# Joining sums and differences of an inverse transform in one VectorE operation per row

## The chip, the cores and the metric

The kernel runs on one core of a Trainium2 chip. The metric is the device time of one execution in microseconds (us), on that core. The core has five engines that work side by side, each through its own queue of instructions in order, and that wait for each other by semaphores: TensorE (PE in the profile, its weight loads PEld), VectorE (DVE), ScalarE (ACT), GpSimd (POOL) and SyncE (SP, which here only issues loads). [...]

## The reference

The kernel computes a long convolution by a gated unit behind it, for a batch of 4, 12800 positions and 128 channels:

```python
u = x * v
y = irfft(rfft(u, n=2*S) * rfft(h_filt, n=2*S))[:, :S, :]
x = x * y
gate_pre[:, t] = sum(conv_w[k] * xp[:, t + k] for k in range(5))   # xp: x with 4 zeros ahead
out = (sigmoid(gate_pre) * (x @ w_val)) @ w_out
```

`h_filt` is a filter that a small network makes from `pos_emb`, times a falling exponential. All values are 32-bit floats.

## The kernel before

The 12800 positions are laid out as J = 2 halves of N1 = 100 by N2 = 64. A position is `n1 * 64 + n2`, and a **row** is one `n2` of one half: 4 batches times 100 positions `n1` (400 elements) for each of the 128 channels. The work has three phases. The first transforms the input along `n1`, the second transforms along `n2`, multiplies with the filter's spectrum and transforms back along `n2` (its results go to the DRAM tensors `c_y` and `c_z`), and the third, which is what the change touches, transforms back along `n1` and does the gated unit. It starts some 680 us into the execution.

In the third phase the 128 rows are worked on in 32 groups of R = 4. The rows pass through these steps, each a small function:

- `y_sum` (L671): two matmuls with the table `inv` give 64 **sums** (S) and 64 **differences** (D) in one PSUM tile `sd`, for two rows at a time.
- `y_copy` (L676): ScalarE copies `sd` to SBUF, `sd_sb`.
- `y_trans` (L683, L685): TensorE transposes it in four pieces (one for each batch) into the PSUM tile `tp`, so that channels lie on the partitions; columns 0 to 63 of a piece are sums, 64 to 127 differences. ScalarE copies the differences, 51 columns of each piece, to `dif` in SBUF.
- `y_join` (L693, L694, L696): VectorE adds, S[i] + D[i] for i = 0 to 50, and subtracts, S[i] - D[i] for i = 1 to 49: a row of 100 values, `yr`. GpSimd multiplies it by the input `xr` and puts it into the tile `ext`.
- `tap` (L710, L713): the convolution over five rows. The first tap is made by ScalarE for a whole group, the four others by VectorE, one for each row of the group, on 1600 elements.
- `sigmoid` (L718), `value` (L725, TensorE, `v_ps`), `gated` (L730, VectorE, `gd`), `project` (L735, TensorE, `o_ps`) and `finish` (L743, ScalarE, `o_sb`, with one store a group).
- `fill_halo` (L651 to L658): ScalarE copies the four rows ahead of a block of four groups into `ext`. For the first block of a half they come from the other end of the signal, moved by one position, so that copy is in pieces.

The order is written out by hand in one loop, one turn for each row. A turn `r` of a group issues: the transposes and the copy of differences of a row that was summed two turns earlier, `value`, the `finish` and `project` of earlier turns, the sums of two rows (every second turn), a tap, a gate, the join, and the copy of a sum; then the halo (r = 1), the next group's first tap (r = 2) or the sigmoid (r = 3). Joins run 8 rows ahead of the taps. The PSUM tiles `tp`, `sd`, `v_ps` and `o_ps` have two buffers each, `dif` and `sd_sb` three, `yr` two.

The positions of a row are not in natural order: `_ORDER` on the host puts 0 to 50 first and then 99 down to 51, as the sums and differences give them, and the host undoes it behind the run.

Of the kernel before, what the change touches and what calls it, by code (L numbers as in the profile page):

```python
# [9 lines left out]
F32 = mybir.dt.float32  # L10
F32R = mybir.dt.float32r
I32 = mybir.dt.int32
AF = mybir.ActivationFunctionType
ALU = mybir.AluOpType
# [9 lines left out]
B, S, D, FO, KC = 4, 12800, 128, 64, 5  # L24
J, N1, N2 = 2, 100, 64
M = N1 * N2
KG = 8
NH = N1 // 2
P0 = 64 - NH
R = 4  # L30
NC1 = N1 // 2 + 1
# [5 lines left out]
def _tables():  # L37
    n1, n2 = np.arange(N1), np.arange(N2)
    k1, k2 = np.arange(N1), np.arange(N2)
    th = 2 * np.pi * (np.outer(n1, 4 * k1 + 1) % (4 * N1)) / (4 * N1)  # L40
    fwd = np.stack([np.cos(th), np.sin(th), -np.cos(th)], 1)

    inv = np.zeros((N1, 3, N2))
    inv[:, 0, :NC1] = (np.cos(th.T) + np.sin(th.T))[:, :NC1] / (2 * M)
    inv[:, 1, :NC1] = (np.cos(th.T) - np.sin(th.T))[:, :NC1] / (2 * M)
    inv[:, 2] = -inv[:, 1]
    flat, inv = inv, np.zeros((128, 3, N2))
    inv[SPREAD] = flat
    ph = (np.outer(4 * k1 + 1, 2 * n2 + 1 - N2)[:, :, None] + 4 * N1 * np.outer(2 * n2 + 1 - N2, k2)[None]) % (8 * M)
    ph = 2 * np.pi * ph / (8 * M)  # L50
    turn = 2 * np.pi * ((N1 - 1) * (4 * k1 + 1) % (8 * N1)) / (8 * N1)

    cos, sin = np.cos(ph[:, :N2 // 2]), np.sin(ph[:, :N2 // 2])
    f = np.stack([np.stack([cos, -sin], 2), np.stack([sin, cos], 2)], 1).reshape(N1, 2 * N2, N2)

    wr, wi = np.cos(ph), np.sin(ph)
    g = np.stack([np.stack([-wi, wr], 1), np.stack([wr, wi], 1)], 2)
    g = g.reshape(N1, 2, 2, 2, N2 // 2, N2).transpose(0, 1, 5, 3, 2, 4).reshape(N1, 2 * N2, 2 * N2)

    ce = 2 * np.pi * ((2 * np.arange(NH)[:, None] + 1 - N1) * (4 * k1 + 1)[None] % (8 * N1)) / (8 * N1)  # L60
    sd = np.zeros((128, 2, 128))
    sd[SPREAD[:, None], :, SPREAD[None]] = np.stack([np.cos(ce), np.sin(ce)], 2)[ROWS[:, 1]]


    f = f.reshape(N1 // 2, 2, 2 * N2, N2).transpose(2, 0, 1, 3).reshape(2 * N2, N1 // 2, 1, 2 * N2)
    g = g.reshape(N1 // 2, 2, 2, N2, 2 * N2).transpose(1, 3, 0, 2, 4).reshape(2 * N2, N1 // 2, 2, 2 * N2)
    w = np.concatenate([f, g], 2)
    be = 2 * np.pi * (np.outer(n2, k2) % N2) / N2
    cb, sb = np.cos(be), np.sin(be)
    dft = np.stack([np.block([[cb, sb], [-sb, cb]]), np.block([[-sb, cb], [-cb, -sb]])], 1)  # L70
    al = 2 * np.pi * np.outer(n2, 4 * k1 + 1) / (4 * M) + turn + np.pi / 4
    tw = np.sqrt(2) * np.tile(np.stack([np.cos(al), np.sin(al)], 1), (2, 1, 1))
    win = np.exp(-0.01 * np.arange(S, dtype=np.float32)).reshape(J, N1, N2)
    win = np.transpose(win, (1, 0, 2))
    tabs = {"fwd": fwd, "sd": sd, "inv": inv, "w": w, "dft": dft, "tw": tw, "win": win, "ident": np.eye(128)}
    return {k: np.ascontiguousarray(a, dtype=np.float32) for k, a in tabs.items()}
# [41 lines left out]
def tile_longconv_gate(  # L118
# [20 lines left out]
    nc = tc.nc  # L139
# [13 lines left out]
    inv = const.tile([128, 3, N2], F32, name="inv")  # L153
# [308 lines left out]
    with tc.tile_pool(name="p2", bufs=1, reuse_waits="tile") as p2, \  # L462
# [89 lines left out]
        with tc.manual_schedule():  # L552
            for p in range(-1, NP + 2):
                now, nxt, old = 0 <= p < NP, p + 1 < NP, 0 <= p - 1 < NP
                if p < 0:
# [6 lines left out]
                    for _ in range(10):  # L562
                        w_ps = ps2.tile([128, 2, BD], F32, name="c_ps", bufs=2)
                        nc.tensor.matmul(
                            out=w_ps[:, 0, 0:2 * D], lhsT=ident, rhs=dft.rearrange("p a k -> p (a k)"), start=True, stop=True)
# [5 lines left out]
                if now:  # L571
                    h = filt_p.pop(p)
# [40 lines left out]
    with tc.tile_pool(name="p3", bufs=1, reuse_waits="tile") as p3, \  # L613
            tc.tile_pool(name="ps3", bufs=1, space=PSUM, reuse_waits="tile") as ps3:
        HALO = KC - 1
# [5 lines left out]
        tails, exts, loads3, sds, tps, gate_sg, gate_gt, outs3 = {}, {}, {}, {}, {}, {}, {}, {}  # L621
# [14 lines left out]
        def place(j, g):  # L636

            if g == NG - 1 and (j, g // EG) not in exts:
                return tails[j], 0
            return exts[j, g // EG], HALO + g % EG * R  # L640
# [5 lines left out]
        def fill_halo(j, q):  # L646
            e = exts[j, q]
            if q == 0:
                t, m = tails[j], N1 // 2
                if j == 0:  # L650
                    nc.vector.memset(e[:, 0:HALO, :, 0:1], 0.0)  # L651
                else:
                    nc.scalar.copy(out=e[:, 0:HALO, :, 0:1], in_=tails[j - 1][:, :, :, m + 1:m + 2])
                nc.scalar.copy(out=e[:, 0:HALO, :, 1:m + 1], in_=t[:, :, :, 0:m])
                nc.scalar.copy(out=e[:, 0:HALO, :, m + 1:N1 - 1], in_=t[:, :, :, m + 2:N1])
                nc.scalar.copy(out=e[:, 0:HALO, :, N1 - 1:N1], in_=t[:, :, :, m:m + 1])
            else:
                nc.scalar.copy(out=e[:, 0:HALO], in_=exts[j, q - 1][:, EG * R:])  # L658

# [19 lines left out]
        def y_trans(s, r):  # L679
            t = sds.pop((s, r))  # L680
            tp = ps3.tile([D, B, 128], F32, name="tp3", bufs=2)
            for b in range(B):
                nc.tensor.transpose(out=tp[:, b], in_=t[:, b], identity=ident)  # L683
            dif = p3.tile([D, B, NC1], F32, name="dif", bufs=3)
            nc.scalar.copy(out=dif, in_=tp[:, :, N2:N2 + NC1])  # L685
            tps[s, r] = tp, dif

        def y_join(s, r):
            tp, dif = tps.pop((s, r))
            j, g = y_order[s]  # L690
            xr = loads3[s].rearrange("d (n b a) -> d n b a", n=R, b=B)[:, r]
            yr = p3.tile([D, B, N1], F32, name="yr", bufs=2)
            nc.vector.tensor_tensor(yr[:, :, 0:NC1], tp[:, :, 0:NC1], dif, op=ALU.add)  # L693
            nc.vector.tensor_tensor(yr[:, :, NC1:N1], tp[:, :, 1:NC1 - 1], dif[:, :, 1:NC1 - 1], op=ALU.subtract)  # L694
            e, r0 = place(j, g)
            nc.gpsimd.tensor_tensor(e[:, r0 + r], yr, xr, op=ALU.mult)  # L696

# [68 lines left out]
        with tc.manual_schedule():  # L766
# [10 lines left out]
            for i in range(-LEAD, (NT - 1) * R):  # L777
                t, r = divmod(i, R)
                s, q = divmod(i + LEAD, R)
                if q == 0 and s < NT:  # L780
                    if 3 <= s + 1 < NT:
                        load_rows(s + 1, (0, 1, 2))
                    j, g = y_order[s]
# [5 lines left out]
                if done:  # L789
                    y_trans(*done)  # L790
# [10 lines left out]
                if done:  # L801
                    y_join(*done)
# [3 lines left out]
                if t + 1 >= 0:  # L806
                    j, g = groups[t + 1]
                    if r == 0 and g == NG - 1:
                        nc.scalar.copy(out=exts[j, g // EG][:, EG * R:], in_=tails[j])
                    if r == 1 and g % EG == 0:  # L810
                        fill_halo(j, g // EG)
                    if r == 2:
                        tap(t + 1, 0)
# [3 lines left out]
            t = NT - 1  # L817
# [24 lines left out]
_INS = ["pos_emb", "w1", "w2", "moe_w_val", "moe_conv_w", "moe_w_out"]  # L842

_OUTS = [((J, D, N2, B, N1), "float32")]
_ORDER = np.concatenate([np.arange(NC1), np.arange(N1 - 1, NC1 - 1, -1)])

# [32 lines left out]
```

## Time and profile before

| | us |
|---|---|
| median of 3 runs | 1068.43 (1066.77 to 1068.98) |
| the profiled execution, by its own time | 1070.6 |
| its span in the trace | 1068.8 |

| engine | busy us | share of the span |
|---|---|---|
| TensorE | 980.4 | 92% |
| VectorE | 972.3 | 91% |
| GpSimd | 747.6 | 70% |
| ScalarE | 624.9 | 58% |

The profile is of one execution. A row of a timeline has the start in us from the start of the span, the length in us, the engine, the line, the operation, what it writes and reads, the size and the count, and in brackets how long the engine sat idle before and what released it. A row of a group has the line, the engine, the operation, the count, then the busy time in us, the mean length in ns, and the idle time before. A row of stretches has, for each engine, its busy us and its instructions, then TensorE's granted clock, the share of the DMA engines and GB/s. An instruction's length includes its way through the engine, so that records of two that follow each other overlap; what a queue can do is read from start to start.

### The profile page before, as it was taken

To read this page: it belongs to the slowest core of one execution; us is meant where nothing else is said; L and a number is where in the kernel's file an instruction comes from. 1 tells how busy PE (TensorE), PEld (TensorE's weight loads), DVE (VectorE), ACT (ScalarE), POOL (GpSimd) and SP (SyncE) were. 2 spreads that over 40 slices of the span, in tenths; PEclk is the share of its full clock that TensorE was granted. 3 is DMA by queue.
4 is the path that set the end of the run, shared out by engine and by line. 5 is a ranking of instruction groups with operands and counts; after the bars stand their busy time and mean duration, and the time that the engine had idled before them with its cause. 6 is when DMAs were issued, how large, how long until landed. Compare 5 with 4: busy or idle time off the path is not lost. (4 is left out here: it accounts for less than half of the span.)

```text
span 1068.8 us, 21559 instructions
## 1 busy us (share of the span) xinstructions
PE 980.4 (92%) x8100; PEld 510.5 (48%) x8100; DVE 972.3 (91%) x1061; ACT 624.9 (58%) x1017; POOL 747.6 (70%) x465
## 2 busy tenths in 40 slices
PE   2768799989998999999999999679999999999996
PEld 0344466656644555455445545334444444444442
DVE  8868999599948999999989999279999999999997
ACT  1545477788862444444434444267677777777774
POOL 2223222222225999999999999689999999999990
PEclk9889899999998999999999999899999999999999
DMA  8999899998989899989989988977788888888813
GB/s 276 372 347 378 329 370 374 384 344 326 388 279 309 317 330 332 334 313 337 344 309 331 345 319 272 342 293 264 273 293 312 270 296 300 278 300 285 298 70 123
DMA packets 97151, 330.16 MB, mean 309 GB/s; under 512 B 12690, under 2 KB 37882, under 8 KB 81050
## 3 DMA queue, kind: packets, MB, share of 16 engines
q1 hardware_dynamic: 41864, 196.96, 54.4%
q10 hardware_dynamic: 49506, 111.30, 26.8%
q0 software_dynamic: 5680, 20.53, 5.0%
q8 instruction: 66, 1.08, 0.4%
q14 instruction: 35, 0.29, 0.1%
HBM read 197.67 MB, written 131.07 MB: 308 GB/s over the span
## 5 line engine op out<-in xcount | busy, mean ns | idle before, releaser
L696 POOL TENSOR_TENSOR ext<-yr,xr 128x400 f32<-128x400 f32 x120 | 308.3, 2570 | 27.3 <-DVE yr L694 24.0
L713 DVE SCALAR_TENSOR_TENSOR gt<-ext,cw,gt 128x1600 f32<-128x1600 f32 (+1 forms) x132 | 240.8, 1824 | 0.1
L400 POOL DMA_DIRECT2D a_u<-st x62 | 33.2, 536 | 225.8 <-ACT st L392 222.0
L392 ACT COPY st<-fp 128x1024 f32<-128x1024 f32 x124 | 125.9, 1030 | 85.4 <-PE fp L391 46.4
L542 POOL TENSOR_TENSOR c_both<-c_raw 128x512 f32<-128x512 f32 x100 | 126.5, 1295 | 9.2 <-DMA c_z<-c_both 6.2
L671 PE MATMUL sd<-ld,inv 128*64 128x512 f32 x512 | 126.4, 612 | 7.2 <-DMA ld<-c_y 6.9
L497 DVE TENSOR_TENSOR va<-z_ps,h_sb 128x2048 f32<-128x2048 f32 x50 | 114.0, 2280 | 18.3 <-PE z_ps L491 18.2
L578 POOL TENSOR_TENSOR va<-va,vb 128x1024 f32<-128x1024 f32 x49 | 117.1, 2390 | 19.0 <-DVE vb L497 18.9
L535 ACT COPY c_raw<-c_ps 128x1024 f32<-128x1024 f32 x50 | 50.8, 1015 | 134.5 <-PE c_ps L530 118.1
L497 DVE TENSOR_TENSOR vb<-z_ps,h_sb 128x2048 f32<-128x2048 f32 x50 | 114.2, 2283 | 11.6 <-POOL va L581 11.6
L676 ACT COPY sd_sb<-sd 128x512 f32<-128x512 f32 x128 | 75.9, 593 | 74.0 <-PE sd L671 62.1
L491 PE MATMUL z_ps<-ld,ld 64*64 64x512 f32 x800 | 111.1, 612 | 8.7 <-DVE vb L497 4.9
L735 PE MATMUL o_ps<-gd,wout 128*128 128x400 f32 x256 | 111.4, 517 | 8.3 <-DVE gd L730 6.8
L391 PE MATMUL fp<-ld,fsd 64*128 64x512 f32 x320 | 90.4, 670 | 28.5 <-DVE ld L342 14.8
L725 PE MATMUL v_ps<-ext,wval 128*128 128x400 f32 x252 | 105.3, 500 | 0.0
L581 POOL TENSOR_TENSOR va<-va,vb 128x1024 f32<-128x1024 f32 x42 | 101.2, 2409 | 0.0
L507 PE MATMUL c_ps<-va,ld 64*64 64x512 f32 x800 | 97.7, 601 | 3.3 <-DVE va L578 1.4
L683 PEld LDWEIGHTS tp<-ident,sd_sb 128*128 128x128 f32 x512 | 58.6, 141 | 77.0 <-PE sd L671 49.6
L513 ACT COPY c_sb<-c_ps 128x1024 f32<-128x1024 f32 x49 | 49.7, 1013 | 58.5 <-PE c_ps L507 58.5
L683 PE MATMUL tp<-ident,sd_sb 128*128 128x128 f32 x512 | 80.3, 280 | 3.8 <-DVE yr L694 2.7
L735 PEld LDWEIGHTS o_ps<-gd,wout 128*128 128x128 f32 x256 | 42.7, 189 | 58.5 <-ACT sd_sb L676 15.4
L730 DVE TENSOR_TENSOR gd<-v_ps,sg 128x400 f32<-128x400 f32 x126 | 70.1, 556 | 0.2 <-ACT sg L718 0.2
(116 smaller groups left out, 1808.8 us busy)
## 6 DMA issues: line engine op xcount, KB each, us to landing
ld<-a_u SPq DMA_DIRECT2D x48, 1024.0 KB
a_u<-st ACTq DMA_DIRECT2D x61, 512.0 KB
xr<-in_xt_dram SPq DMA_DIRECT2D x32, 800.0 KB
c_y<-c_sb ACTq DMA_DIRECT2D x49, 512.0 KB
out_dram<-o_sb ACTq DMA_DIRECT2D x31, 800.0 KB
c_z<-c_both ACTq DMA_DIRECT2D x48, 512.0 KB
ld<-in_xv_dram SPq DMA_DIRECT2D x40, 512.0 KB
ld<-c_y SPq DMA_DIRECT2D x32, 512.0 KB
```

What stands on the lines that cost most here:

```text
L392: nc.scalar.copy(out=st[:, c], in_=fp.rearrange("k j e -> k (j e)"))
L491: nc.tensor.matmul(out=z[half[h], c], lhsT=wk[half[c], 0, half[h]], rhs=a2[half[c], h, j], start=True, stop=True)
L497: nc.vector.tensor_tensor(out, z.rearrange("p (b d) -> p b d", d=D).unsqueeze(1).to_broadcast([128, n, B, D]), h_sb.unsqueeze(2).to_broadc ...
L542: nc.gpsimd.tensor_tensor(both[:, :, m], raw[:, :, 1], raw[:, :, 0], op=op)
L578: (nc.gpsimd if nxt else nc.vector).tensor_tensor(va[:, 0:2], va[:, 0:2], vb[:, 0:2], op=ALU.add)
L581: nc.gpsimd.tensor_tensor(va[:, 2:4], va[:, 2:4], vb[:, 2:4], op=ALU.add)
L671: nc.tensor.matmul(out=to, lhsT=inv[:, 2 if j * m * c else c], rhs=t, start=True, stop=True)
L683: nc.tensor.transpose(out=tp[:, b], in_=t[:, b], identity=ident)
L696: nc.gpsimd.tensor_tensor(e[:, r0 + r], yr, xr, op=ALU.mult)
L713: nc.vector.scalar_tensor_tensor(gt, rows(t, k)[:, cols], cw[:, k:k + 1], gt, op0=ALU.mult, op1=ALU.add)
L725: nc.tensor.matmul(out=v_ps, lhsT=wval, rhs=rows(t)[:, r * ROW:(r + 1) * ROW], start=True, stop=True)
L735: nc.tensor.matmul(out=o_ps, lhsT=wout, rhs=gd, start=True, stop=True)
```

## The change

The differences are copied twice by ScalarE: columns 0 to 49 as they are, and columns 1 to 50 with the sign changed. VectorE then makes the row of 100 in one addition. It reads 50 sums twice over, the second time one column further on, by an access pattern with a step of one column between the two halves, and adds the two halves of `dif`. A row now holds S[i] + D[i] for i = 0 to 49 and S[i] - D[i] for i = 1 to 50. Position 50 therefore comes from a difference instead of a sum, so the table `inv` has the sign of its difference turned, its place in a row is the last (`_ORDER`), and the pieces of the halo's copies are cut one column earlier.

```diff
     inv[:, 1, :NC1] = (np.cos(th.T) - np.sin(th.T))[:, :NC1] / (2 * M)
+    inv[:, 1, NH] *= -1
     inv[:, 2] = -inv[:, 1]
...
-                    nc.scalar.copy(out=e[:, 0:HALO, :, 0:1], in_=tails[j - 1][:, :, :, m + 1:m + 2])
-                nc.scalar.copy(out=e[:, 0:HALO, :, 1:m + 1], in_=t[:, :, :, 0:m])
-                nc.scalar.copy(out=e[:, 0:HALO, :, m + 1:N1 - 1], in_=t[:, :, :, m + 2:N1])
-                nc.scalar.copy(out=e[:, 0:HALO, :, N1 - 1:N1], in_=t[:, :, :, m:m + 1])
+                    nc.scalar.copy(out=e[:, 0:HALO, :, 0:1], in_=tails[j - 1][:, :, :, m:m + 1])
+                nc.scalar.copy(out=e[:, 0:HALO, :, 1:m], in_=t[:, :, :, 0:m - 1])
+                nc.scalar.copy(out=e[:, 0:HALO, :, m:N1 - 1], in_=t[:, :, :, m + 1:N1])
+                nc.scalar.copy(out=e[:, 0:HALO, :, N1 - 1:N1], in_=t[:, :, :, m - 1:m])
...
-            dif = p3.tile([D, B, NC1], F32, name="dif", bufs=3)
-            nc.scalar.copy(out=dif, in_=tp[:, :, N2:N2 + NC1])
+            dif = p3.tile([D, B, 2, NH], F32, name="dif", bufs=3)
+            nc.scalar.copy(out=dif[:, :, 0], in_=tp[:, :, N2:N2 + NH])
+            nc.scalar.activation(dif[:, :, 1], tp[:, :, N2 + 1:N2 + NC1], AF.Copy, scale=-1.0)
...
-            nc.vector.tensor_tensor(yr[:, :, 0:NC1], tp[:, :, 0:NC1], dif, op=ALU.add)
-            nc.vector.tensor_tensor(yr[:, :, NC1:N1], tp[:, :, 1:NC1 - 1], dif[:, :, 1:NC1 - 1], op=ALU.subtract)
+            sums = tp[:, :, 0:NH]
+            twice = bass.AP(sums.tensor, sums.offset, [*sums.ap[:2], (1, 2), sums.ap[2]])
+            nc.vector.tensor_tensor(yr.rearrange("d b (h a) -> d b h a", h=2), twice, dif, op=ALU.add)
...
-_ORDER = np.concatenate([np.arange(NC1), np.arange(N1 - 1, NC1 - 1, -1)])
+_ORDER = np.concatenate([np.arange(NH), np.arange(N1 - 1, NC1 - 1, -1), [NH]])
```

In VectorE's queue, in the middle of the third phase, two rows of the signal stand like this before the change (the number behind `tp` names the row's buffer):

```order
L693 TENSOR_TENSOR yr<-tp_6592,dif 128x4x51
L694 TENSOR_TENSOR yr<-tp_6592,dif 128x4x49
L713 SCALAR_TENSOR_TENSOR gt<-ext,cw,gt 128x1600
L730 TENSOR_TENSOR gd<-v_ps,sg 128x400
L693 TENSOR_TENSOR yr<-tp_6622,dif 128x4x51
L694 TENSOR_TENSOR yr<-tp_6622,dif 128x4x49
```

and with the change, where lines of the code are numbered three higher or so, like this, with the next row's join:

```order
L697 TENSOR_TENSOR yr<-tp_6592,dif 128x400
L716 SCALAR_TENSOR_TENSOR gt<-ext,cw,gt 128x1600
L733 TENSOR_TENSOR gd<-v_ps,sg 128x400
L697 TENSOR_TENSOR yr<-tp_6622,dif 128x400
L716 SCALAR_TENSOR_TENSOR gt<-ext,cw,gt 128x1600
L733 TENSOR_TENSOR gd<-v_ps,sg 128x400
L697 TENSOR_TENSOR yr<-tp_6645,dif 128x400
```

One instruction a row is gone; tap and gate stand as before. In ScalarE's queue the turns r = 2 and r = 3 of the same group are, before,

```order
L685 COPY dif<-tp_6592 128x204
L743 COPY o_sb<-o_ps 128x400
L676 COPY sd_sb<-sd 128x512
L710 ACTIVATE gt<-ext,cw 128x1600
L685 COPY dif<-tp_6622 128x204
L743 COPY o_sb<-o_ps 128x400
L676 COPY sd_sb<-sd 128x512
L718 ACTIVATE sg<-gt 128x1600
```

and with the change

```order
L686 COPY dif<-tp_6592 128x4x50
L687 ACTIVATE dif<-tp_6592 128x4x50
L746 COPY o_sb<-o_ps 128x400
L677 COPY sd_sb<-sd 128x512
L713 ACTIVATE gt<-ext,cw 128x1600
L686 COPY dif<-tp_6622 128x4x50
L687 ACTIVATE dif<-tp_6622 128x4x50
L746 COPY o_sb<-o_ps 128x400
L677 COPY sd_sb<-sd 128x512
L721 ACTIVATE sg<-gt 128x1600
```

Each row has one instruction more, right behind the first copy and ahead of the copies of the projection and of the sums. The orders on TensorE, GpSimd and SyncE are the same.

## The prediction

> **What bounds the kernel now.** The whole-span shares do not tell which engine to speed up, since three are near full. The stretch in which the changed lines run does. I first read busy time by stretches of the span, and the groups of that stretch:
>
> ```profile
> core 0: us, PE busy (x) PEld busy (x) DVE busy (x) ACT busy (x) POOL busy (x), PEclk, DMA share, GB/s
> 720.00:1031.00 311.00, 311.00 (x1323) 144.39 (x1324) 311.00 (x441) 228.57 (x397) 287.55 (x111) 1.00 0.80 278
> L713 DVE SCALAR_TENSOR_TENSOR gt<-ext,cw,gt 128x1600 f32<-128x1600 f32 x111 | 206.9, 1864 | 0.0
> L693 DVE TENSOR_TENSOR yr<-tp,dif 128x204 f32<-128x204 f32 x110 | 38.4, 349 | 0.0
> ```
>
> TensorE and VectorE are both busy for all 311 us, in which 110 rows are joined; ScalarE has 82 us left, and VectorE is idle 0.0 us before its groups. Only one of the two full engines can be the pace. The timeline decides; in it one row of VectorE's work is
>
> ```profile
> 852.19 1.86 DVE L713 SCALAR_TENSOR_TENSOR gt<-ext,cw,gt 128x1600 f32<-128x1600 f32 x1
> 853.98 0.56 DVE L730 TENSOR_TENSOR gd<-v_ps,sg 128x400 f32<-128x400 f32 x1
> 854.46 0.35 DVE L693 TENSOR_TENSOR yr<-tp,dif 128x204 f32<-128x204 f32 x1
> 854.74 0.34 DVE L694 TENSOR_TENSOR yr<-tp,dif 128x196 f32<-128x196 f32 x1
> 855.01 1.86 DVE L713 SCALAR_TENSOR_TENSOR gt<-ext,cw,gt 128x1600 f32<-128x1600 f32 x1
> ```
>
> Records overlap, so I count from start to start: tap 1.79, gate 0.48, joins 0.28 and 0.27, together 2.82 us. Each follows the one before by its own length less 0.07 to 0.08: nothing is waited for. VectorE's row is 2.82 us by its own work. TensorE's two rows in the same place are
>
> ```profile
> 852.58 0.50 PE L725 MATMUL v_ps<-ext,wval 128*128 128x400 f32 x1
> 852.91 0.83 PE L735 MATMUL o_ps<-gd,wout 128*128 128x400 f32 x2
> 853.58 0.60 PE L683 MATMUL tp<-ident,sd_sb 128*128 128x128 f32 x4
> 854.02 0.84 PE L725 MATMUL v_ps<-ext,wval 128*128 128x400 f32 x2
> 854.69 0.90 PE L735 MATMUL o_ps<-gd,wout 128*128 128x400 f32 x2
> 855.52 1.94 PE L671 MATMUL sd<-ld,inv 128*64 128x512 f32 x8
> 857.39 0.66 PE L683 MATMUL tp<-ident,sd_sb 128*128 128x128 f32 x4
> ```
>
> Two rows take 5.65 us here too, with no gap, but one of the two projections (`o_ps`) is longer: 0.90 against 0.83 for the same shape. The long one, at 854.69, needs the `gd` that VectorE finished at 853.98 + 0.56 = 854.54; the short one, at 852.91, needs a `gd` that ended a microsecond before. So TensorE is held some 0.06 us in every pair by VectorE, and it hides in a record's length. That this is a hold and not TensorE's own time is shown where it is held in the open:
>
> ```profile
> 716.28 0.94 PE L735 MATMUL o_ps<-gd,wout 128*128 128x400 f32 x2 [0.57 <-DVE gd L730]
> 717.05 0.60 PE L683 MATMUL tp<-ident,sd_sb 128*128 128x128 f32 x4
> 719.10 0.94 PE L735 MATMUL o_ps<-gd,wout 128*128 128x400 f32 x2 [0.77 <-DVE gd L730]
> 719.97 0.65 PE L671 MATMUL sd<-ld,inv 128*64 128x512 f32 x2
> ```
>
> A projection that waits is followed by transposes after 0.77 us, against 0.67 when it doesn't wait (852.91 to 853.58): 0.10 for the late start. Followed by `sd` it takes 0.87 when it waits, so 0.77 when it doesn't; at 854.69 it takes 0.83. VectorE is the pace, and TensorE alone would need 5.65 - 0.06 = 5.59 us for two rows, 2.79 for one. **The second bound lies 0.03 us a row behind the first.**
>
> **The change, part by part.** TensorE, GpSimd and the queue of loads keep their order.
>
> VectorE: two joins of 51 and 49 columns times 4 (0.28 + 0.27) become one of 400 elements. The trace has no such operation, and the nearest row is the gate at 853.98: the same 400 elements from PSUM and SBUF, 0.48 us. From above it is bounded by the two joins' 0.55 (the same elements, one start less), from below by the 0.28 of the larger half. I take the gate's 0.48: elements cost alike in both, and cutting the elements into four runs (854.46) shows no price, as 204 and 400 elements then stand at about 1.02 ns each with 0.07 left over. Row: 1.79 + 0.48 + 0.48 = 2.75, a saving of 0.065 (the rounded rows give 0.07, TensorE's pair 0.06).
>
> This saving is not the kernel's, because TensorE's 2.79 is then late. VectorE gets ahead, the hold of 0.06 a pair goes within a pair or two, and from there the pair takes 5.59. In the stretch of 110 rows these are 55 pairs: 55 x 0.06 = **3.3 us**. VectorE can also use up its lag behind TensorE, since the end of the kernel hangs on its taps. How much, ScalarE's rows tell:
>
> ```profile
> 868.45 1.63 ACT L710 ACTIVATE gt<-ext,cw 128x1600 f32<-128x1600 f32 x1
> 869.98 0.32 ACT L685 COPY dif<-tp 128x204 f32<-128x204 f32 x1
> 870.19 0.50 ACT L743 COPY o_sb<-o_ps 128x400 f32<-128x400 f32 x1
> 870.57 0.61 ACT L676 COPY sd_sb<-sd 128x512 f32<-128x512 f32 x1
> 871.40 0.35 DVE L693 TENSOR_TENSOR yr<-tp,dif 128x204 f32<-128x204 f32 x1
> 871.63 0.90 PE L735 MATMUL o_ps<-gd,wout 128*128 128x400 f32 x2
> ```
>
> This is the latest `dif` of a group of four rows, as it stands behind the 1.53 us of a first tap: it ends at 870.30, 1.10 before its join. ScalarE's next instruction starts 0.21 after a copy of this size, so the second copy ends 0.2 to 0.33 later, and 0.8 to 0.9 are left. The gate's `v_ps` leaves as much (852.58 + 0.50 = 853.08, gate at 853.98). I take **0.8 us**. A negated copy instead of a plain one costs nothing here:
>
> ```profile
> L479 ACT ACTIVATE h_sb<-c_ps 128x256 f32<-128x256 f32 x50 | 20.1, 402 | 0.0
> L480 ACT COPY h_sb<-c_ps 128x256 f32<-128x256 f32 x50 | 19.6, 391 | 0.0
> ```
>
> It takes 402 ns where the copy takes 391. In the stretch ScalarE's 110 added copies cost 110 x 0.21 = 23 us of its 82 idle ones. What covers them is that `sd_sb` waits for TensorE every second row; without this cover they would delay `o_sb`, which empties a buffer that TensorE needs two projections on, by 0.2 to 0.4, against 0.9 of slack (`o_sb` of 870.19 ends at 870.69, TensorE writes that buffer again at 871.63).
>
> The cover is missing at the start of the phase, where ScalarE works without a gap and the others wait for it:
>
> ```profile
> 698.00 0.33 ACT L685 COPY dif<-tp 128x204 f32<-128x204 f32 x1 [0.84 <-PE tp L683]
> ...
> 700.33 0.34 ACT L685 COPY dif<-tp 128x204 f32<-128x204 f32 x1
> ...
> 702.56 0.34 ACT L685 COPY dif<-tp 128x204 f32<-128x204 f32 x1
> 703.00 0.37 DVE L693 TENSOR_TENSOR yr<-tp,dif 128x204 f32<-128x204 f32 x1 [1.60 <-ACT dif L685]
> 703.72 12.91 POOL L696 TENSOR_TENSOR ext<-yr,xr 128x400 f32<-128x400 f32 x5 [1.20 <-DVE yr L694]
> ```
>
> Three second copies stand in this chain, 0.63 us, less 0.08 for the join that ends sooner. GpSimd's gapless chain of five products behind it hands the delay on: **-0.55 us**. (0 if it is absorbed, 1 if each copy costs its full 0.33.)
>
> [...]
>
> The moved column (51 and 49 columns of the halo copies become 50 and 50, a table's sign, the host's order) keeps counts and sizes: 0.
>
> At the end TensorE has no `sd` left and waits for VectorE in the open:
>
> ```profile
> 1030.54 1.94 PE L671 MATMUL sd<-ld,inv 128*64 128x512 f32 x8
> 1040.99 0.91 PE L735 MATMUL o_ps<-gd,wout 128*128 128x400 f32 x2 [1.24 <-DVE gd L730]
> ```
>
> In these 10.4 us lie the last four joins, one for each 2.82, and there the whole saving counts: 4 x 0.065 = 0.25. Sum: 3.3 + 0.8 - 0.55 + 0.25 = 3.8 us. The profiled execution took 1070.6 us (span 1068.8), which becomes 1066.8; it was 2.2 above the median of the runs, 1068.43, which becomes **1064.6**.
>
> **Rivals.** *VectorE stays the pace*, if TensorE has slack that I don't see: 110 x 0.065 - 0.55 + 0.25 = 6.9, 1061.5. For it: every wait shown in the open is TensorE's for VectorE. Against: the pair of rows above shows no other place where TensorE is held. GpSimd stands near this case:
>
> ```profile
> 852.34 2.61 POOL L696 TENSOR_TENSOR ext<-yr,xr 128x400 f32<-128x400 f32 x1 [0.20 <-DVE yr L694]
> 701.48 1.04 POOL L696 TENSOR_TENSOR ext<-yr,xr 128x400 f32<-128x400 f32 x1 [1.29 <-DVE yr L694]
> 708.47 2.11 DVE L713 SCALAR_TENSOR_TENSOR gt<-ext,cw,gt 128x1600 f32<-128x1600 f32 x1
> ```
>
> Its product takes 1.04 alone and 2.61 under a tap, ending 0.97 after the tap (854.95); where it runs late, the tap is stretched to 2.11. A tap that had to wait for it would make the row 1.79 + 0.97 = 2.76, still under 2.79: it takes 1 us from this rival, nothing from the forecast. [...]
>
> *No change*: TensorE's 0.83 before `sd` is its own, so its pair stays 5.65. Then 0.8 + 0.25 - 0.55 = 0.5 is left, 1067.9. For it: no unheld projection ahead of `sd` is in the trace. Against: 0.77 and 0.87 above.
>
> *Slower*: the join's new reading of the sums, twice over with an offset of one column, in eight runs of 50, costs something at each run. VectorE then becomes the pace from a join of 0.55 on, at (0.55 - 0.48) / 8 = 9 ns a run. At twice that the join is 0.62, the row 2.89, and 110 x 0.07 + 0.55 makes 8 us: 1076.7. For it: no row has such a reading. Against: four runs cost nothing at 854.46.
>
> **How the numbers follow.** Forecast (1063 to 1066.3) 0.60, VectorE's pace 0.10, no change 0.19, slower 0.11. About 0.2%, 2.1 us, can be told from no change in a measurement: faster 0.70, same 0.19, slower 0.11. The range runs from VectorE's pace with a little more, 1061.0, to no change at 1067.9; beyond lie the slower case and half of no change, 0.2.
>
> **What would show it.** Right: one join a row, the gate's 0.56 long; TensorE's projection 0.83 long in both rows and its pair at 5.59; VectorE with small idle times before joins or gates (on `dif` or `v_ps`), where it had none; 703.72's product half a microsecond later. Wrong: projections that still alternate 0.83 and 0.90 (VectorE's pace), a pair still at 5.65 though VectorE idles (no change), a join of over 0.62 long (slower).

## The result, and the profile after

| | before | with the change |
|---|---|---|
| median of 12 runs each, us | 1069.32 | 1064.09 |
| ratio, 95% interval | | 0.9948 [0.9934, 0.9963] |
| profiled execution, us (span) | 1070.6 (1068.8) | 1066.5 (1064.7) |

The kernel is faster by 0.4 to 0.7%. The two profiled executions lie 4.1 us apart. The groups of VectorE in the same stretch of the third phase (line, engine, operation, count, busy us, mean ns, idle us before):

```profile
L716 DVE SCALAR_TENSOR_TENSOR gt<-ext,cw,gt 128x1600 f32<-128x1600 f32 x113 | 212.1, 1877 | 0.0
L733 DVE TENSOR_TENSOR gd<-v_ps,sg 128x400 f32<-128x400 f32 x112 | 63.5, 567 | 0.0
L697 DVE TENSOR_TENSOR yr<-tp,dif 128x400 f32<-128x400 f32 x112 | 63.4, 566 | 0.6 <-ACT dif L687 0.3 <-ACT o_sb L746 0.2
```

The single join is as long as the gate, 566 against 567 ns. The 311 us from 716 on now hold 112 joins, where the same length held 110. VectorE looks as full as before: it is idle 0.6 us. TensorE's timeline, in the middle of the phase, tells what happened:

```profile
850.70 0.66 PE L684 MATMUL tp<-ident,sd_sb 128*128 128x128 f32 x4
851.19 0.84 PE L728 MATMUL v_ps<-ext,wval 128*128 128x400 f32 x2
851.86 0.83 PE L738 MATMUL o_ps<-gd,wout 128*128 128x400 f32 x2
852.54 0.60 PE L684 MATMUL tp<-ident,sd_sb 128*128 128x128 f32 x4
852.97 0.84 PE L728 MATMUL v_ps<-ext,wval 128*128 128x400 f32 x2
853.65 0.83 PE L738 MATMUL o_ps<-gd,wout 128*128 128x400 f32 x2
854.41 1.94 PE L672 MATMUL sd<-ld,inv 128*64 128x512 f32 x8
856.28 0.44 PE L684 MATMUL tp<-ident,sd_sb 128*128 128x128 f32 x2
```

Both projections are 0.83 long, the one ahead of `sd` takes 0.76 from start to start where it took 0.83, and the pair of rows takes 856.28 - 850.70 = 5.58 us instead of 5.65. No projection in it is held any more: TensorE is the pace, as E3 below shows. VectorE, whose row needs 1.80 + 0.48 + 0.48 = 2.76 (taps at 850.32 and 853.08), now waits for the rest of 2.79, and the waits fall into the overlap of its records, as here (a turn with ScalarE behind a first tap):

```profile
857.65 0.57 DVE L733 TENSOR_TENSOR gd<-v_ps,sg 128x400 f32<-128x400 f32 x1
857.78 0.35 ACT L687 ACTIVATE dif<-tp 128x200 f32<-128x200 f32 x1
858.24 0.57 DVE L697 TENSOR_TENSOR yr<-tp,dif 128x400 f32<-128x400 f32 x1
858.73 1.87 DVE L716 SCALAR_TENSOR_TENSOR gt<-ext,cw,gt 128x1600 f32<-128x1600 f32 x1
```

The join stands 0.59 behind the gate instead of 0.48, since the second copy ends only at 858.13. The profile counts no idle time, as the gate's record reaches to 858.22. Only the distance from start to start shows such a wait.

Where the 4.05 us that these two profiles differ by in the third phase come from can be read at five points: the fifth pair of sums (2.89 us behind the fourth in both), the first tap, the joins of the 13th, the 37th and the 125th row, and the end of the span. Before:

```profile
698.29 1.94 PE L671 MATMUL sd<-ld,inv 128*64 128x512 f32 x8
703.56 1.87 DVE L713 SCALAR_TENSOR_TENSOR gt<-ext,cw,gt 128x1600 f32<-128x1600 f32 x1
716.15 0.35 DVE L693 TENSOR_TENSOR yr<-tp,dif 128x204 f32<-128x204 f32 x1
783.89 0.35 DVE L693 TENSOR_TENSOR yr<-tp,dif 128x204 f32<-128x204 f32 x1
1032.31 0.35 DVE L693 TENSOR_TENSOR yr<-tp,dif 128x204 f32<-128x204 f32 x1
```

and with the change:

```profile
698.25 1.94 PE L672 MATMUL sd<-ld,inv 128*64 128x512 f32 x8
704.10 1.87 DVE L716 SCALAR_TENSOR_TENSOR gt<-ext,cw,gt 128x1600 f32<-128x1600 f32 x1
716.68 0.56 DVE L697 TENSOR_TENSOR yr<-tp,dif 128x400 f32<-128x400 f32 x1
782.88 0.56 DVE L697 TENSOR_TENSOR yr<-tp,dif 128x400 f32<-128x400 f32 x1
1028.47 0.57 DVE L697 TENSOR_TENSOR yr<-tp,dif 128x400 f32<-128x400 f32 x1
```

| part, us | before | after | difference |
|---|---|---|---|
| fifth pair of sums to first tap | 703.56 - 698.29 = 5.27 | 704.10 - 698.25 = 5.85 | +0.58 |
| first tap to join 13 | 12.59 | 12.58 | 0.0 |
| join 13 to join 37 | 67.74 | 66.20 | -1.54 |
| join 37 to join 125 | 248.42 | 245.59 | -2.83 |
| join 125 to the end | 36.5 | 36.2 | -0.3 |

Between the joins of rows 13 and 125 the change wins 4.37 us, in two parts. For the first 24 rows VectorE goes at its own pace, 66.20 / 24 = 2.758 us a row: it uses up its lag behind TensorE. From there on it goes at TensorE's, 245.59 / 88 = 2.791. Before, a row took 2.823 all along. At 2.791 from the start the 112 rows would have won 3.6 us; the faster first 24 add 0.8.

### The profile page after: what moved, and what is told of

It reads as the page before. It is cut to its first block, busy times and chain, and to the rows that moved or that the text cites. A ratio compares the mean times of both kernels' runs of the same rounds, so it can differ in the third digit from the quotient of the medians.

```text
span 1064.7 us, 21554 instructions
## 1 busy us (share of the span) xinstructions
PE 978.8 (92%) x8100; PEld 515.6 (48%) x8100; DVE 966.9 (91%) x933; ACT 649.2 (61%) x1145; POOL 747.9 (70%) x465
## 4 chain that ended last, share of the span: by engine, by line
PE 65%; DMA 13%; DVE 7%; POOL 5%; ACT 4%; issue 4%; SPq 1%; ACTq 1%; DVEq 0%; POOLq 0%
PE sd L672 11%; PE o_ps L738 8%; PE v_ps L728 7%; PE c_ps L531 7%; PE fp L392 6%; PE tp L684 6%; PE c_ps L508 6%; PE z_ps L492 5%; DMA xv<-in_xv_dram 4%; DMA ld<-in_xv_dram 3%; PE gp L293 3%; PE ap L267 3%; DMA c_z<-c_both 2%; DVE vb L498 2%; POOL c_both L543 2%
## 5 line engine op out<-in xcount | busy, mean ns | idle before, releaser
L738 PE MATMUL o_ps<-gd,wout 128*128 128x400 f32 x256 | 107.8, 503 | 6.1 <-DVE gd L733 4.6
L697 DVE TENSOR_TENSOR yr<-tp,dif 128x400 f32<-128x400 f32 x128 | 72.5, 566 | 25.8 <-ACT dif L687 21.6
```

Source lines behind the costliest of these rows:

```text
L738: nc.tensor.matmul(out=o_ps, lhsT=wout, rhs=gd, start=True, stop=True)
```

## The experiments

The kernels' instructions do not differ ahead of the third phase, yet in the profiles the fifth pair of sums starts anywhere between 694.46 and 702.97 us. That is the size of the scatter of whole times, and larger than most effects here. So the table has, beside the ratios, what the changed code sets: the time from the fifth pair of sums to the end of the span (the rest), and the steady time of two rows on TensorE. The rest is read from one profile of each kernel; the two profiles of the change agree in it within 0.1 us. Where transposes are added or narrowed, the steps from pair to pair ahead of the fifth are some 0.1 us longer or shorter too, which the rest leaves out. An experiment's ratio is against runs of the kernel before on the same chip, and comes from 12 runs of its own kernel (E5: 5, E7 and E9: 6); E5 to E8 ran on one chip, the other experiments on another.

| kernel | fifth pair, us | span, us | rest, us | pair, us | ratio to before |
|---|---|---|---|---|---|
| before | 698.29 | 1068.8 | 370.5 | 5.65 | 1 |
| the change | 698.25 | 1064.7 | 366.4 | 5.58 | 0.9948 [0.9934, 0.9963] |
| E1 copies only | 700.10 | 1071.3 | 371.2 | 5.65 | 1.0013 [0.9989, 1.0038] |
| E2 one copy | 694.46 | 1060.2 | 365.7 | 5.58 | 0.9970 [0.9950, 0.9991] |
| E3 more transposes, after | 702.97 | 1075.5 | 372.5 | 5.69 | 1.0030 [1.0006, 1.0054] |
| E4 more transposes, before | 698.77 | 1071.0 | 372.2 | 5.69 | 1.0031 [1.0009, 1.0052] |
| E5 narrow transposes | 696.68 | 1060.4 | 363.7 | 5.52 | 0.9906 [0.9886, 0.9926] |
| E6 start on VectorE | 701.33 | 1069.0 | 367.7 | 5.58 | 0.9978 [0.9957, 0.9999] |
| E7 both | 696.59 | 1061.4 | 364.8 | 5.52 | 0.9941 [0.9920, 0.9961] |
| E8 the change again | 700.81 | 1067.3 | 366.5 | 5.58 | 0.9960 [0.9943, 0.9976] |
| E9 narrow, eight rows | 699.40 | 1062.9 | 363.5 | 5.52 | 0.9920 [0.9896, 0.9944] |
| E10 narrow transposes, before | 699.12 | 1069.7 | 370.6 | 5.65 | 0.9990 [0.9972, 1.0008] |

All ratios but one agree with the rest. E5's puts it some 10 us under before, its rest 6.8, which lies outside the ratio's interval; where the other 3 us come from is not shown.

**E1: ScalarE's half alone.**

```diff
-            nc.vector.tensor_tensor(yr.rearrange("d b (h a) -> d b h a", h=2), twice, dif, op=ALU.add)
+            nc.vector.tensor_tensor(yr[:, :, 0:NH], tp[:, :, 0:NH], dif[:, :, 0], op=ALU.add)
+            nc.vector.tensor_tensor(yr[:, :, NH:N1], tp[:, :, 1:NC1], dif[:, :, 1], op=ALU.add)
```

> Only the change's ScalarE half is made: both copies of the differences, but the join stays two VectorE additions (4x50 elements each). Theory (VectorE's row is the pace before, TensorE stands 0.03 us a row behind it, ScalarE's copies are covered in steady state): the row stays 2.82 us, the pair of rows 5.65, TensorE's projections still alternate 0.83 and 0.90; only the start costs, about 0.6 us, so 0 to 1 us slower than before. Rival (ScalarE's second copy lies on the path in steady state): each of 110 rows would cost up to 0.21 us, 23 us, or at least the two turns of a group with a tap or a sigmoid 2 x 0.21, 12 us.

The rest of the span is 0.7 us longer than before. TensorE's rows alternate as before:

```profile
849.78 0.83 PE L737 MATMUL o_ps<-gd,wout 128*128 128x400 f32 x2
...
851.56 0.90 PE L737 MATMUL o_ps<-gd,wout 128*128 128x400 f32 x2
...
855.42 0.83 PE L737 MATMUL o_ps<-gd,wout 128*128 128x400 f32 x2
...
857.20 0.90 PE L737 MATMUL o_ps<-gd,wout 128*128 128x400 f32 x2
```

ScalarE's second copies cost nothing in steady state: the pair is 5.65 with and without them. What they cost, they cost at the start: the first tap stands 706.05 - 700.10 = 5.95 us behind the fifth pair of sums, 0.68 later than before. The rival with 12 to 23 us is out.

**E2: VectorE's half alone.**

```diff
-            nc.scalar.activation(dif[:, :, 1], tp[:, :, N2 + 1:N2 + NC1], AF.Copy, scale=-1.0)
...
+            nc.vector.tensor_tensor(yr.rearrange("d b (h a) -> d b h a", h=2), twice, dif[:, :, 0:1].to_broadcast([D, B, 2, NH]), op=ALU.add)
```

> The change's VectorE half without ScalarE's second copy: the one addition reads the 50 plain differences twice (the sign of the second half is left out, so the second half of each row is not what the reference has). Theory (TensorE is the pace after the change): the pair of rows stays 5.58 us as with the change, and only the start is 0.5 us earlier, so 0.5 us faster than the change, 4 to 6 us faster than before. Rival (ScalarE's second copy holds VectorE back after the change): the row falls to VectorE's own 2.76, the pair to 5.52, 2.5 to 3.5 us faster than the change.

The rest is 0.7 us shorter than with the change, too little for the ratios to tell. It is won at the start, where the first tap stands 699.61 - 694.46 = 5.15 us behind the fifth pair, against 5.85. The pair stays where the change has it, at 5.59 by these two rows (5.58 over many):

```profile
851.80 0.66 PE L684 MATMUL tp<-ident,sd_sb 128*128 128x128 f32 x4
857.39 0.66 PE L684 MATMUL tp<-ident,sd_sb 128*128 128x128 f32 x4
```

So after the change it is not ScalarE's second copy that keeps VectorE from its 2.76; without it the pair is no shorter.

**E3 and E4: one transpose more in every second row**, with the change and without it.

```diff
+            if r % 2:
+                nc.tensor.transpose(out=tp[:, 3], in_=t[:, 3], identity=ident)
```

> The changed kernel with one more transpose (0.11 us on TensorE, the same data written twice) in every second row. Theory (TensorE is the pace after the change): every added microsecond counts, pair 5.58 + 0.11 = 5.69, 55 x 0.11 = 6.0 us slower than the change, about as slow as before. Rival (VectorE or ScalarE is the pace after the change, TensorE has slack): at most 2 us slower than the change.

> The kernel before with the same added transpose of 0.11 us in every second row. Theory (TensorE is held 0.06 us in each pair by VectorE): the first 0.06 is covered by the hold, the projection's 0.90 becomes 0.83, pair 5.58 + 0.11 = 5.69 instead of 5.65, 55 x 0.045 = 2.5 us slower than before. Rival 1 (no hold, TensorE is already the pace at 5.65): 55 x 0.11 = 6.0 us slower. Rival 2 (TensorE has more slack than the hold): no change.

E3's rest is 372.5 - 366.4 = 6.1 us longer than the change's, every added 0.11 us counted. E4, without the change, has the same pair of 5.69, and in the timeline the hold is gone:

```profile
850.62 0.83 PE L737 MATMUL o_ps<-gd,wout 128*128 128x400 f32 x2
851.38 1.94 PE L671 MATMUL sd<-ld,inv 128*64 128x512 f32 x8
853.25 0.66 PE L683 MATMUL tp<-ident,sd_sb 128*128 128x128 f32 x4
853.74 0.27 PE L685 MATMUL tp<-ident,sd_sb 128*128 128x128 f32 x1
...
854.53 0.83 PE L737 MATMUL o_ps<-gd,wout 128*128 128x400 f32 x2
...
856.31 0.83 PE L737 MATMUL o_ps<-gd,wout 128*128 128x400 f32 x2
857.07 1.51 PE L671 MATMUL sd<-ld,inv 128*64 128x512 f32 x6
```

The kernel before took 0.04 us of the added 0.11 into its pair, the rest went into the hold: this is the 0.06 to 0.07 that the prediction read from a record's length. The rest of the span is only 1.7 us longer, under the expected 2.5, because VectorE works off its lag of 0.8 us here too, a term that the expectation had left out: it still takes 67.73 us from the join of row 13 to that of row 37, as before the change, and slows to 2.845 a row only some ten rows later.

**E5 and E10: narrower transposes**, with the change and without it. The columns behind the last difference are not transposed.

```diff
-                nc.tensor.transpose(out=tp[:, b], in_=t[:, b], identity=ident)
+                nc.tensor.transpose(out=tp[:, b, 0:115], in_=t[0:115, b], identity=ident[0:115, 0:115])
```

> The changed kernel with transposes of 115 instead of 128 columns (the columns behind the last difference are not used). Theory (TensorE at 5.58 a pair is the pace after the change, VectorE's own row of 2.76 is right behind it): a transpose falls from 0.109 to about 0.098, the pair by 8 x 0.011 = 0.09 to 5.49, so VectorE becomes the pace again at 2.76 a row, its pair 5.52 with a projection of 0.90 in every second row; from the 30th joined row or so on 0.03 a row is won, 2.5 to 3 us faster than the change. Rival (GpSimd is next, its product ends 0.97 after a tap): row 2.77, 2 us faster than the change. Rival (ScalarE's late second copy): no gain.

> The kernel before with transposes of 115 columns. Theory (VectorE's row of 2.82 is the pace before): pair stays 5.65, the 0.09 taken from TensorE becomes a longer hold, no gain (third phase within 0.3 us of before). Rival (TensorE's work is the pace before): 55 x 0.09 = 5 us faster.

The same edit on TensorE gives 366.4 - 363.7 = 2.7 us with the change and nothing without it (370.6 against 370.5). That is the plainest sign of which engine is the pace on either side. In E10 the time saved goes into a longer wait: the projection that is held takes 0.84 from start to start where 0.77 is its own, and the `v_ps` ahead of it 0.73 instead of 0.68. In E5 VectorE's row is its own work again:

```profile
850.32 0.57 DVE L697 TENSOR_TENSOR yr<-tp,dif 128x400 f32<-128x400 f32 x1
850.80 1.88 DVE L716 SCALAR_TENSOR_TENSOR gt<-ext,cw,gt 128x1600 f32<-128x1600 f32 x1
852.60 0.57 DVE L733 TENSOR_TENSOR gd<-v_ps,sg 128x400 f32<-128x400 f32 x1
853.08 0.57 DVE L697 TENSOR_TENSOR yr<-tp,dif 128x400 f32<-128x400 f32 x1
```

with 2.76 from join to join. One part of the expectation did not come: TensorE's projections are 0.83 in both rows, none is held, and its pair fell to 5.52 and not to 5.49:

```profile
853.33 0.61 PE L684 MATMUL tp<-ident,sd_sb 115*128 115x115 f32 x4
853.77 0.85 PE L728 MATMUL v_ps<-ext,wval 128*128 128x400 f32 x2
854.46 0.83 PE L738 MATMUL o_ps<-gd,wout 128*128 128x400 f32 x2
855.13 0.56 PE L684 MATMUL tp<-ident,sd_sb 115*128 115x115 f32 x4
855.53 0.85 PE L728 MATMUL v_ps<-ext,wval 128*128 128x400 f32 x2
856.21 0.50 PE L738 MATMUL o_ps<-gd,wout 128*128 128x400 f32 x1
```

From start to start the two groups of transposes take 0.44 + 0.40 here and 0.49 + 0.43 with the change, 0.08 less; but the two `v_ps` behind them take 1.37 instead of 1.35. That leaves the 0.06 by which the pair fell. The two engines now stand within 0.01 us a row of each other, and which of them is the last to give way there remains open.

**E6, E7, E9: the start.** The second copies of the first rows go to VectorE, which is idle there (with the change 0.37 to 1.96 us ahead of each join from 695.68 to 703.60): ten rows (E6), the same with narrow transposes (E7), eight rows with narrow transposes (E9, where the condition is `if s < 2:`).

```diff
-            nc.scalar.activation(dif[:, :, 1], tp[:, :, N2 + 1:N2 + NC1], AF.Copy, scale=-1.0)
+            if s < 2 or (s, r) in ((2, 0), (2, 1)):
+                nc.vector.tensor_scalar(out=dif[:, :, 1], in0=tp[:, :, N2 + 1:N2 + NC1], scalar1=-1.0, scalar2=None, op0=ALU.mult)
+            else:
+                nc.scalar.activation(dif[:, :, 1], tp[:, :, N2 + 1:N2 + NC1], AF.Copy, scale=-1.0)
```

> The changed kernel, but the second copy of the first ten rows is made by VectorE (a multiplication by -1 from PSUM), which is idle there. Theory (the start costs 0.55 us by ScalarE's three second copies): the first tap comes as early behind the fifth pair of sums as before the change (5.3 us instead of 5.85), 0.5 us faster than the change; steady state unchanged at 5.58. Rival (the start is set by GpSimd or TensorE): no gain.

> Both: transposes of 115 columns, and the second copy of the first ten rows on VectorE. Theory: both gains add, 3 to 3.5 us faster than the change, 7 to 9 us faster than before (ratio to before 0.992 to 0.993).

E6 was a miss, and so was E7: E6's rest is 1.3 us longer than the change's, and E7's 1.1 longer than E5's. E6's first tap stands 707.21 - 701.33 = 5.88 us behind the fifth pair, no earlier than the change's 5.85, and from there the start takes longer. The timeline shows why:

```profile
706.44 0.57 DVE L700 TENSOR_TENSOR yr<-tp,dif 128x400 f32<-128x400 f32 x1
706.94 0.36 DVE L688 TENSOR_SCALAR dif<-tp 128x200 f32<-128x200 f32 x1
707.10 1.03 POOL L702 TENSOR_TENSOR ext<-yr,xr 128x400 f32<-128x400 f32 x1 [1.19 <-DVE yr L700]
707.21 2.60 DVE L719 SCALAR_TENSOR_TENSOR gt<-ext,cw,gt 128x1600 f32<-128x1600 f32 x1
709.74 0.56 DVE L700 TENSOR_TENSOR yr<-tp,dif 128x400 f32<-128x400 f32 x1
```

The copy for the ninth row stands between a join and a tap. In that time GpSimd's product starts, 0.11 us ahead of the tap, and the tap takes 2.60 instead of 1.87. The extra 0.73 is most of the 0.92 that the product still runs (to 708.13), and the product takes 1.03, no longer than it does alone (1.04): by these rows it is the tap that waits. The next one does too: it takes 2.60 at 710.49, 0.11 behind its product. With the tap right behind the join it is the tap that comes first, and the product that waits: with the change the first tap, at 704.10, takes 1.87, and the five products from 704.26 on take 12.91, 2.58 each. That costs less: with the change such a row takes 2.58 us from join to join (705.89 to 708.47), here 3.30 (706.44 to 709.74).

> Transposes of 115 columns, and VectorE makes the second copy of the first eight rows only, so that no such copy stands between a join and a tap. Theory (with ten rows the copy let GpSimd's product start 0.1 us ahead of two taps, which then waited 0.7 us each): no tap at the start is longer than 1.88 before GpSimd runs without a gap, the first tap stands 5.3 to 5.5 us behind the fifth pair of sums, third phase 0.3 to 0.5 us shorter than with narrow transposes alone, ratio to before 0.992. Rival (VectorE's copy itself delays the start): no shorter than with narrow transposes alone.

With eight rows no tap at the start is so stretched (the first three take 1.88, 2.18 and 2.18), and the rest is 363.5, E7's 364.8 less 1.3. Against narrow transposes alone that is 0.2 us, half of what was expected; the first tap stands 5.65 us behind the fifth pair, not 5.3 to 5.5, since VectorE's own copy now lies in front of the join (the copy starts at 704.09, the join at 704.55). What caused the miss is shown: without the copy between join and tap the taps of 2.60 are gone. The worth of the cure, 0.2 us, is too small for the ratios to tell.

**E8: the change once more.**

> The changed kernel once more, beside the three above on one chip. Theory: 3.8 to 4.3 us faster than before (ratio 0.996), the pair of rows 5.58, the same third phase as in the first profile to 0.3 us. Rival (the 5.6 us of the first comparison are the size of the gain, with something won outside the third phase): ratio 0.9945 to 0.995 again.

Its rest is that of the first profile to 0.1 us, 4.0 us under before, and its ratio is 0.9960 with an interval that holds 4.0 us (0.9962). The first comparison's 5.6 us have 4.0 at the edge of their interval; what the excess is, is not shown. 4 us is what both profiles show the change to do.

## Why the prediction was right

- *VectorE is the pace before, TensorE 0.03 us a row behind it.* Shown from both sides: taking 0.06 us off TensorE's pair (0.09 had been expected) changes nothing before (E10), and adding 0.11 costs only 0.04 a pair (E4). The second bound had been read from a record that is 0.90 instead of 0.83 long.
- *The join costs what the gate costs, 0.48.* Right: 566 and 567 ns, 0.48 from start to start. Reading the sums twice in eight runs cost nothing here; the slower case is out.
- *TensorE becomes the pace, pair 5.59.* 5.58 was measured, steadily; E3 and E5 show it.
- *3.3 us from the pair and 0.8 from VectorE's lag*, 4.1 in all: 3.6 and 0.8 between the joins of rows 13 and 125, where the pace changes after 24 rows.
- *0.25 at the end*: 0.3. *0.55 lost at the start*: 0.58, and E1 and E2 place it with ScalarE's second copies (the first tap 0.68 later with them alone, 0.70 earlier without them).
- *Sum 3.8*: 4.05 in the profiles. The first comparison's 5.6 us are more; the profiles show nothing of the excess of 1.5 in the third phase, and E8 did not repeat it.
- *The time of 1064.6* is nearer to the measured 1064.09 than its working earns. It starts from 1068.43, the median of the three runs known then, where the twelve have 1069.32: the same 3.8 us taken off that give 1065.5. That it came within half a microsecond is luck; the parts of the sum are borne out one by one above.
- *ScalarE's copies are covered elsewhere.* Right by E1 (pair 5.65 with the second copies, as before) and E2 (5.58 without them, as with the change). That VectorE would in some turns wait for `dif` was right too (858.24 above), but it costs nothing, since the pair is no shorter without the second copy.

## What to carry to other kernels

When two engines look equally full, the saving on the pacing one is cut off where the other begins (here VectorE's own row fell by 0.065 us to 2.758, the kernel's by 0.032 to 2.791), and how far that is can be read ahead: look for the same operation with two lengths in a steady pattern, since here a short wait showed as a longer record (TensorE, 0.90 against 0.83) or only from start to start (VectorE, 0.59 against 0.48), and not as idle time. A cut on the engine behind was worth nothing until the first had been made: the narrower transposes gave 0 us before and 2.7 us after. And putting an instruction into an idle engine's queue was not free where it stood between a join and a tap: two taps took 2.60 us instead of 1.87, and the rest of E6 is 1.3 us longer than the change's.

## What was not expected of the hardware

- Of VectorE's tap and GpSimd's product it was, in two pairs of rows, the later one that took longer: 0.11 us behind the product a tap took 2.60 us instead of 1.87, and the product 1.03 (E6, 707.10 and 707.21); 0.15 us behind a tap of 1.86 the product took 2.61 instead of 1.04 (before, 852.19 and 852.34). What makes the later one wait is not shown.
- Eight transposes of 115 columns instead of 128 took 0.08 us less from start to start, but the pair fell by 0.06 (5.58 to 5.52), since each `v_ps` behind them took 0.01 more (E5). Why it did is not shown.
